# A packed-attention and two-MoE kernel: the order of the second MoE derived anew, and the sums that close each of its last two thirds moved

## The chip, the cores and the metric

The kernel runs on one core of a Trainium2 chip. The metric is the device time of one execution in microseconds (us), the median of several runs. Five engines work side by side: TensorE (PE, with its weight loads shown as PEld), VectorE (DVE), ScalarE (ACT), GpSimd (POOL) and SyncE (SP), which here only issues transfers (DMAs).

## The reference, cut to what matters

```
attn:  p_packed = softmax(p k^T / 8) v ;  x = softmax(q p_packed^T / 8) p_packed     (4 batches, 8 heads, 576 rows, 64)
moe:   h = x @ w_in ;  x = (h * cos(h)) @ w_out                                       (2304 x 512, d_ff 2048)
moe2:  p = domain_probs / sum ;  out = sum over 4 experts of  p[:, e] * (relu(x @ w1[e]) @ w2[e])    (F = 1024)
```

All of it is float32. To keep that accuracy on TensorE, each operand is split into a high and a low part, and each product is three matmuls (`mm3`, lines 204 to 207: high by high, high by low, low by high).

## The kernel before, in words

The work has two large stages. The first holds attention and the first MoE (up to about 395 us of the span). The second MoE fills the rest: 2304 tokens in three thirds (`NH = 3`), and 8 steps in each (`NU = 8`: 4 experts by 2 halves of 1024), 24 steps in all, numbered n. A step has two pieces on TensorE. `b_pair` (called twice, for j = 0 and 1) makes the hidden block by seven half-size products (`PRODUCTS`, Winograd's scheme), with additions on VectorE (L958), a relu that is multiplied with the experts' shares (L975), differences (L987), and a split into a high part (ACT, L667) and a low part (POOL, or VectorE where the planner puts it there; L658, `split`). The second product is `b_back` in the first third (512 columns to a matmul, evacuated in L1077), and `b_back2` in the other two: again seven products (`BACK`), each of 12 matmuls of 384 columns, named by their pair of operands. They add into five accumulators `v`, `w`, `c11`, `x53` and `x74`, each evacuated by one VectorE instruction over 768 columns (L1134), or by ACT for an accumulator's first product (L1132). w2's blocks that the last two thirds use are copied within the chip's main memory beforehand (`copy_w2`, L1318), since they are loaded again in each step (`kept_weights`).

At the end of a third (`u == NU - 1`), `final` (L1149) makes three sums on VectorE: x53 += v, w += x53, x74 += v, and `put` (L1156) stores c11, x53, w and x74.

The order of every engine's instructions is made by a planner (`Plan.run`). Each operation is entered with its engine, a duration in us, what it comes after, the buffers that it takes and uses, and for TensorE and SP a key. The planner walks through time: of the operations of an engine that can start first, it takes the one with the lowest key, and a TensorE operation whose key is more than 60 (`AHEAD`) above the lowest key left has to wait. A POOL operation with an `alt` can go to VectorE instead. Operations marked `port` and those of POOL never run at once in the plan. What comes out is one fixed list for each engine, and the chip runs each list in order. Three things scale the plan of the second MoE: `pl.slow` multiplies the durations on ACT, VectorE and POOL, `pl.late` is added to each transfer's end, and after a TensorE operation whatever depends on it may start 0.25 us later (`LATENCY`). The keys of a step are an offset of 100 n plus a number from `KEYS`: "a" for the 14 products of the two `b_pair`, "b" for those of `b_back` or `b_back2`, with lists of their own for the first step, the first third ("one"), the middle ("two"), the step before the end ("end") and the last products of all ("last").

Of the kernel before, what the change touches and what calls it, by code (L numbers as in the profile page):

```python
# [15 lines left out]
ALU = mybir.AluOpType  # L16
# [10 lines left out]
class Plan:  # L27
# [35 lines left out]
    def run(self):  # L63
# [15 lines left out]
        while done < len(self.ops):  # L79
# [55 lines left out]
            for x, w in [(x, fin) for x in o["next"]] + [(x, t) for x in o["then"]]:  # L135
                x["wait"] -= 1
                x["at"] = max(x["at"], w)
                if not x["wait"]:
                    todo[x["eng"]].append(x)
# [7 lines left out]
def tile_packed_attention_moe_moe2(ctx: ExitStack, tc: tile.TileContext, qT, kT, vk, pT, w_in, w_out, dp, w1, w2, out, out2):  # L147
# [16 lines left out]
    nc = tc.nc  # L164
# [59 lines left out]
    def dma(us, f, after=(), take=(), use=(), key=None, begun=()):  # L224
        return pl.op("SP", us, f, after, take, use, key, begun=begun)
# [873 lines left out]
    def b_back2(n, W, keys):  # L1099
# [4 lines left out]
        for i, (a, b, bank, new, acc, how) in enumerate(BACK):  # L1104
# [22 lines left out]
            def f_evac(ob=ob, ac=ac, acc=acc, how=how, first=first):  # L1127
                p = ob["t"][:, :, :TB]
# [4 lines left out]
                else:  # L1133
                    nc.vector.tensor_tensor(out=ac["t"], in0=ac["t"] if how == ALU.subtract else p,  # L1134
                                            in1=p if how == ALU.subtract else ac["t"], op=how)

            m = pl.op("PE", 2.08, f_mm, [g["ready"] for g in gl] + [w["ready"] for w in ws] + ([] if new else [free[bank]]),
                      [ob["slot"]] if new else [], [ob["slot"]] + [g["slot"] for g in gl] + [w["slot"] for w in ws], keys[i])
            free[bank] = ac["op"] = pl.op("ACT" if first else "DVE", 0.85 if first else 0.96, f_evac, [m, ac["op"]],
                                          [ac["slot"]] if first else [], [ob["slot"], ac["slot"]], keys[i] + 8)  # L1140
            last[0] = m
        if u < NU - 1:
            return

        def final(x, y, key):
            a, b = accs[h, x], accs[h, y]

            def f():
                nc.vector.tensor_tensor(out=a["t"], in0=a["t"], in1=b["t"], op=ALU.add)  # L1149

            a["op"] = pl.op("DVE", 0.95, f, [a["op"], b["op"]], [], [a["slot"], b["slot"]], key, port=True)

        def put(x, i, c, key):
            def f():
                t0 = (h - 1) * TH + c * TB
                nc.sync.dma_start(out=out2[i * 256:(i + 1) * 256, t0:t0 + TB].rearrange("(d p) n -> p d n", p=P),  # L1156
                                  in_=accs[h, x]["t"])

            dma(0.4 * MB2, f, [accs[h, x]["op"]], [], [accs[h, x]["slot"]], key)

        kf = keys[-1] + 20
        put("c11", 0, 0, kf)
        final("x53", "v", kf + 1), final("w", "x53", kf + 2), final("x74", "v", kf + 3)
        put("x53", 0, 1, kf + 10), put("w", 1, 1, kf + 11), put("x74", 1, 0, kf + 12)

# [9 lines left out]
    def share_ops():  # L1175
# [10 lines left out]
        def f_store():  # L1186
# [11 lines left out]
            'copy': [715.7, 22.6],  # L1198
# [7 lines left out]
            'keep': [117.2, -167, 205.3, 42.6],  # L1206
            'kept': [173.4, 203.5],
            'last': {'b': [39.4, 45.5, 37.7, 357.6, 51.2, 27.5, 165.9]},
# [27 lines left out]
            'one': {'a': [7.9, 13.2, 18.6, 61.7, 42.4, 68.2, 50.5, 39, 15.5, 61.8, 75.1, 71.4, 76.6, 72.1],  # L1236
                    'b': [14.1, 54.6, 76.5, 77.4, 55.9, 66.8]},
            'out0': [-122.9, -853.4],
            'two': {'a': [-11.2, 43, 29.3, 19.8, 20.5, 46.9, 7.1, 23, 52.9, 69, 21.4, 71.4, 100.2, 84.8],
                    'b': [8, 40.1, 58.9, 16.6, 79.4, 52.2, 103.3]}}  # L1240
# [86 lines left out]
    pl.slow, pl.late = 1.04, 0.8  # L1327
# [90 lines left out]
```

## Time and profile before

| what | us |
|---|---|
| median of 3 runs (lowest, highest) | 1152.04 (1151.27, 1152.55) |
| the profiled execution's own time | 1149.58 |
| its span, first to last instruction | 1147.8 |
| TensorE busy in the span | 1101.7 (96%) |
| VectorE, POOL, ACT busy | 835.3, 633.2, 493.4 |

The span is the stretch that the profile covers; the profiled execution took 1.8 us more than it, and 2.46 us less than the median. Busy TensorE time is modelled from the ends of pipelined matmuls, so a busy share near 100% can hide short gaps; how many matmuls start in a stretch tells more. In the lines of the profile, "idle before, releaser" is the time in which the engine stood still ahead of an instruction, and what it had waited for.

### The profile page before, as it was taken

How to read it: one execution, taken by the hardware profiler on the slowest of the kernel's cores; microseconds unless marked ns; L12 is line 12 of the kernel's file. 1: busy time of each engine (PE TensorE's matmuls, PEld its weight loads, DVE VectorE, ACT ScalarE, POOL GpSimd, SP SyncE). 2: the span in 40 equal slices, each digit the busy share in tenths (PEclk: the TensorE clock that was granted, in tenths of full speed). 3: DMA queues.
4: the chain of work that ended last, by engine and by line, in shares of the span. 5: the costliest groups of instructions: out<-in, count | busy, mean ns of one | idle time of the engine just before them, and what ended most of it. 6: DMA issues, size and time to landing. Idle time of an engine off the chain costs nothing.

```text
span 1147.8 us, 19120 instructions
## 1 busy us (share of the span) xinstructions
PE 1101.7 (96%) x7241; PEld 1032.5 (90%) x7241; DVE 835.3 (73%) x1244; ACT 493.4 (43%) x852; POOL 633.2 (55%) x477
## 2 busy tenths in 40 slices
PE   6689999999999999999999999999999999999997
PEld 4568999999999988888888889999999999999997
DVE  3798777567555677787777756888887768778776
ACT  3677655445444453244334434333334343333331
POOL 1454755435422775555566546656667767645553
PEclk8699999999999999999999999999999999999999
DMA  9673436433135859787866967676667876666653
GB/s 314 231 263 118 161 116 266 188 130 141 43 105 188 280 196 325 265 301 256 291 257 263 335 259 249 232 252 233 244 227 249 306 265 238 226 227 219 228 182 110
DMA packets 96815, 257.70 MB, mean 225 GB/s; under 512 B 10892, under 2 KB 34516, under 8 KB 94548
## 3 DMA queue, kind: packets, MB, share of 16 engines
q1 hardware_dynamic: 96724, 256.48, 63.1%
q8 instruction: 57, 0.93, 0.3%
q14 instruction: 34, 0.28, 0.1%
HBM read 192.97 MB, written 71.86 MB: 231 GB/s over the span
## 4 chain that ended last, share of the span: by engine, by line
PE 78%; DVE 8%; DMA 5%; issue 4%; ACT 3%; POOL 2%; SPq 0%; POOLq 0%; ACTq 0%; DVEq 0%
PE pa L205 26%; PE pa L207 25%; PE pa L206 25%; DMA w<-w 3%; PE pa L353 2%; DVE pa L958 1%; DVE s L755 1%; POOL aop L658 1%; POOL w L658 1%; DMA kt<-kT 1%; DVE acc L1134 1%; DVE p L958 1%; DVE u L975 0%; DVE oacc L1077 0%; DVE g L1010 0%
## 5 line engine op out<-in xcount | busy, mean ns | idle before, releaser
L205 PE MATMUL pa<-g,w 128*128 128x288 f32 (+1 forms) x960 | 303.6, 316 | 2.0 <-DVE acc L1134 0.8
L206 PE MATMUL pa<-g,w 128*128 128x288 f32 (+1 forms) x960 | 301.6, 314 | 1.2 <-POOL g L590 1.2
L207 PE MATMUL pa<-g,w 128*128 128x288 f32 (+1 forms) x960 | 301.2, 314 | 0.5 <-POOL w L297 0.5
L658 POOL TENSOR_TENSOR g<-u,g 128x384 fp32r<-128x384 f32 x157 | 171.5, 1105 | 140.3 <-ACT g L667 133.5
L205 PE MATMUL pa<-bop,aop 128*128 128x384 f32 x672 | 228.8, 341 | 9.3 <-DVE p L958 4.1
L207 PE MATMUL pa<-bop,aop 128*128 128x384 f32 x672 | 226.9, 338 | 1.5 <-POOL aop L658 1.5
L206 PE MATMUL pa<-bop,aop 128*128 128x384 f32 x672 | 226.3, 337 | 1.1 <-POOL bop L658 1.1
L205 PEld LDWEIGHTS pa<-g,w 128*128 128x128 f32 x960 | 180.1, 188 | 7.9 <-issue 2.4
L206 PEld LDWEIGHTS pa<-g,w 128*128 128x128 f32 x960 | 180.2, 188 | 1.9 <-POOL g L590 1.9
L207 PEld LDWEIGHTS pa<-g,w 128*128 128x128 f32 x960 | 180.4, 188 | 1.0 <-POOL w L297 1.0
L667 ACT ACTIVATE g<-u 128x384 fp32r<-128x384 f32 x192 | 97.2, 523 | 176.8 <-DVE u L987 134.9
L590 POOL TENSOR_TENSOR g<-t,g 128x576 fp32r<-128x576 f32 x64 | 93.2, 1470 | 118.8 <-ACT g L587 117.4
L205 PEld LDWEIGHTS pa<-bop,aop 128*128 128x128 f32 x672 | 126.1, 188 | 19.1 <-DVE p L958 6.1
L206 PEld LDWEIGHTS pa<-bop,aop 128*128 128x128 f32 x672 | 126.2, 188 | 3.0 <-POOL bop L658 1.4
L207 PEld LDWEIGHTS pa<-bop,aop 128*128 128x128 f32 x672 | 126.1, 188 | 2.2 <-POOL aop L658 2.2
L958 DVE TENSOR_TENSOR p<-pa,p 128x384 f32<-128x384 f32 x144 | 79.3, 554 | 41.4 <-PE pa L207 38.7
L1134 DVE TENSOR_TENSOR acc<-pa,acc 128x768 f32<-128x768 f32 x88 | 83.9, 954 | 32.6 <-PE pa L207 31.3
L658 POOL TENSOR_TENSOR w<-w 128x512 fp32r<-128x512 f32 x62 | 86.3, 1403 | 31.4 <-ACT w L705 31.2
L205 PE MATMUL pa<-at,m 128*128 128x288 f32 x256 | 78.7, 307 | 3.1 <-DVE t L583 2.0
L206 PE MATMUL pa<-at,m 128*128 128x288 f32 x256 | 77.5, 303 | 2.8 <-POOL at L658 2.8
L205 PE MATMUL pa<-w,g 128*128 128x512 f32 x192 | 75.9, 395 | 1.9 <-DVE oacc L1077 1.9
L207 PE MATMUL pa<-at,m 128*128 128x288 f32 x256 | 77.2, 301 | 0.0
(129 smaller groups left out, 1924.8 us busy)
## 6 DMA issues: line engine op xcount, KB each, us to landing
at<-at SPq DMA_DIRECT2D x16, 1152.0 KB, 5.3
raw<-w SPq DMA_DIRECT2D x32, 512.0 KB, 5.2
w<-w SPq DMA_DIRECT2D x64, 256.0 KB, 5.0
raw<-w_in SPq DMA_DIRECT2D x6, 1024.0 KB, 6.1
raw<-w_out SPq DMA_DIRECT2D x6, 1024.0 KB, 8.0
vt<-vk SPq DMA_DIRECT2D x8, 576.0 KB, 8.5
kt<-kT SPq DMA_DIRECT2D x8, 576.0 KB, 10.5
qt<-qT SPq DMA_DIRECT2D x8, 576.0 KB, 8.6
```

Of the source, the lines that this page charges most:

```text
L205: nc.tensor.matmul(o, lhsT=l(0), rhs=r(0), start=first, stop=False, skip_group_check=True)
L206: nc.tensor.matmul(o, lhsT=l(0), rhs=r(1), start=False, stop=False, skip_group_check=True)
L207: nc.tensor.matmul(o, lhsT=l(1), rhs=r(0), start=False, stop=last, skip_group_check=True)
L353: nc.tensor.matmul(o(e)[32 * q:32 * q + 32, :N], lhsT=l[64 * e:64 * e + 64, 32 * q:32 * q + 32], rhs=r(q // 2, q % 2)[64 * e:64 * e + 64], ...
L590: nc.gpsimd.tensor_tensor(out=s["g"][:, 1], in0=s["t"], in1=s["g"][:, 0].bitcast(F32), op=ALU.subtract)
L658: (nc.vector if on_vector else nc.gpsimd).tensor_tensor(out=dst[:, 1], in0=src, in1=dst[:, 0].bitcast(F32), op=ALU.subtract)
L667: nc.scalar.activation(r["t"][:, 0], src(), AF.Copy)
L755: nc.vector.tensor_tensor(out=t, in0=src(a, m)(), in1=src(b, m)(), op=o)
L958: nc.vector.tensor_tensor(out=s[o] if o in s else tmp(o), in0=s[x], in1=s[y], op=ALU.add)
L1134: nc.vector.tensor_tensor(out=ac["t"], in0=ac["t"] if how == ALU.subtract else p, in1=p if how == ALU.subtract else ac["t"], op=how)
```

## The change

Three things are edited. In the planner, a TensorE operation that depends on another TensorE operation may start as soon as that one's duration is over, without the 0.25 us, in the second MoE (`o["fair"]`). `pl.slow` goes from 1.04 to 1.08. And in `b_back2`, for the last step of a third, the sums and stores are entered in another place: c11 is stored after its last product (i = 2); after i = 5 come x74 += v, x53 += v, the store of x53, w += x53 and the store of w; the last entry, a22 by t4 (i = 6), is then added to x74 in two halves of 384 columns, each stored by itself. The keys of the second MoE and those of `copy`, `keep`, `kept` and `g` are new numbers. (Unchanged entries of `load` are left out below.)

```diff
--- before.py
+++ after.py
@@ -132,7 +132,7 @@
                 s["end"] = max(s["end"], fin)
                 if not s["users"]:
                     ends[s["tag"]].append(s["end"])
-            for x, w in [(x, fin) for x in o["next"]] + [(x, t) for x in o["then"]]:
+            for x, w in [(x, t + us if o["fair"] and eng == "PE" == x["eng"] else fin) for x in o["next"]] + [(x, t) for x in o["then"]]:
                 x["wait"] -= 1
                 x["at"] = max(x["at"], w)
                 if not x["wait"]:
@@ -1124,44 +1124,52 @@
                             return ws[0]["t"][:, x, k, d * P:(d + 1) * P]
                         mm3(ob["t"][:, d, :TB], l, lambda x: gl[k]["t"][:, x], new and k == 0, k == 1)
 
-            def f_evac(ob=ob, ac=ac, acc=acc, how=how, first=first):
-                p = ob["t"][:, :, :TB]
+            def f_evac(d=slice(0, 2), ob=ob, ac=ac, acc=acc, how=how, first=first):
+                p = ob["t"][:, d, :TB]
                 if first:
                     ac["t"] = (bp["ys"].tile([P, 2, TB], F32, tag="ys", name="acc", bufs=5) if acc == "x53" else
                                bp["raw"].tile([P, 2, 512], F32, tag="raw", name="acc", bufs=4)[:, :, :TB])
                     nc.scalar.activation(ac["t"], p, AF.Copy, scale=-1.0 if how == ALU.subtract else 1.0)
                 else:
-                    nc.vector.tensor_tensor(out=ac["t"], in0=ac["t"] if how == ALU.subtract else p,
-                                            in1=p if how == ALU.subtract else ac["t"], op=how)
+                    o = ac["t"][:, d]
+                    nc.vector.tensor_tensor(out=o, in0=o if how == ALU.subtract else p, in1=p if how == ALU.subtract else o,
+                                            op=how)
 
             m = pl.op("PE", 2.08, f_mm, [g["ready"] for g in gl] + [w["ready"] for w in ws] + ([] if new else [free[bank]]),
                       [ob["slot"]] if new else [], [ob["slot"]] + [g["slot"] for g in gl] + [w["slot"] for w in ws], keys[i])
+            last[0] = m
+            if u == NU - 1 and i == 6:
+                for d in range(2):
+                    ac["op"] = pl.op("DVE", 0.56, lambda d=d, f=f_evac: f(slice(d, d + 1)), [m, ac["op"]], [],
+                                     [ob["slot"], ac["slot"]], keys[i] + 8)
+                    put(h, acc, 1, 0, keys[i] + 12, d)
+                continue
             free[bank] = ac["op"] = pl.op("ACT" if first else "DVE", 0.85 if first else 0.96, f_evac, [m, ac["op"]],
                                           [ac["slot"]] if first else [], [ob["slot"], ac["slot"]], keys[i] + 8)
-            last[0] = m
-        if u < NU - 1:
-            return
-
-        def final(x, y, key):
-            a, b = accs[h, x], accs[h, y]
-
-            def f():
-                nc.vector.tensor_tensor(out=a["t"], in0=a["t"], in1=b["t"], op=ALU.add)
-
-            a["op"] = pl.op("DVE", 0.95, f, [a["op"], b["op"]], [], [a["slot"], b["slot"]], key, port=True)
-
-        def put(x, i, c, key):
-            def f():
-                t0 = (h - 1) * TH + c * TB
-                nc.sync.dma_start(out=out2[i * 256:(i + 1) * 256, t0:t0 + TB].rearrange("(d p) n -> p d n", p=P),
-                                  in_=accs[h, x]["t"])
-
-            dma(0.4 * MB2, f, [accs[h, x]["op"]], [], [accs[h, x]["slot"]], key)
-
-        kf = keys[-1] + 20
-        put("c11", 0, 0, kf)
-        final("x53", "v", kf + 1), final("w", "x53", kf + 2), final("x74", "v", kf + 3)
-        put("x53", 0, 1, kf + 10), put("w", 1, 1, kf + 11), put("x74", 1, 0, kf + 12)
+            if u == NU - 1 and i == 2:
+                put(h, "c11", 0, 0, keys[i] + 20)
+            if u == NU - 1 and i == 5:
+                final(h, "x74", "v", keys[i] + 9), final(h, "x53", "v", keys[i] + 10)
+                put(h, "x53", 0, 1, keys[i] + 20)
+                final(h, "w", "x53", keys[i] + 11)
+                put(h, "w", 1, 1, keys[i] + 21)
+
+    def final(h, x, y, key):
+        a, b = accs[h, x], accs[h, y]
+
+        def f():
+            nc.vector.tensor_tensor(out=a["t"], in0=a["t"], in1=b["t"], op=ALU.add)
+
+        a["op"] = pl.op("DVE", 0.95, f, [a["op"], b["op"]], [], [a["slot"], b["slot"]], key, port=True)
+
+    def put(h, x, i, c, key, d=None):
+        def f():
+            t0 = (h - 1) * TH + c * TB
+            dst = out2[i * 256:(i + 1) * 256, t0:t0 + TB].rearrange("(d p) n -> p d n", p=P)
+            t = accs[h, x]["t"]
+            nc.sync.dma_start(out=dst if d is None else dst[:, d], in_=t if d is None else t[:, d])
+
+        dma((0.4 if d is None else 0.2) * MB, f, [accs[h, x]["op"]], [], [accs[h, x]["slot"]], key)
 
     last, last_out = [None], [None]
 
@@ -1195,17 +1203,17 @@
                     [-93.3, -128.7, -68.2, -15.3, 13.3, 1421.4], [-83.4, 135.4, 82.9, 153.5, 102.6, 397.7]],
             'b': [[-144.5, 19.2, -205.9, -87.6], [-87.2, -44.5, 18, 62.9], [6.2, 37.5, 59.6, 71.8]],
             'blk': [206.7, 346.1, 218.8, 569.5, 339.1],
-            'copy': [715.7, 22.6],
-            'end': {'a': [1.9, 33.8, -41.8, -9.4, 62.6, 50.5, 58.2, 66, 50.3, 65.2, 164.6, 90.7, 98.5, 108.6],
-                    'b': [15.2, 19.6, 61.8, 6.4, -4.3, 137.2, 95.6]},
+            'copy': [698.4, -92.8],
+            'end': {'a': [7.4, 49.9, -96.8, -25.8, 10, 20.2, 59.3, 66, 69.2, 67.3, 153, 123.2, 167.4, 107.5],
+                    'b': [0.5, 22.1, 43, 35.4, -0.2, 147.4, 142.3]},
             'f': [[-837.7, -739.1, -526.4, -725.8], [-47.1, 45.5, 49.7, 46.5], [-3, 19.7, 90.8, 30.6],
                   [-10.1, 23.9, 43.8, 42.1]],
-            'first': {'a': [-99.6, -21.7, -44.8, 52.4, 61.8, -13.5, 44, -18.2, -13.9, 59.1, 88.2, 109.3, 65.9, 52.5]},
-            'g': [40.4, 18.4],
+            'first': {'a': [-115.8, -35.2, -26.6, 46, 88.4, 27.1, 37.9, 1.5, 6.9, 75.4, 52, 130.5, 41.1, 64.9]},
+            'g': [32.9, 10.4],
             'in0': [-1061.7, -368.5],
-            'keep': [117.2, -167, 205.3, 42.6],
-            'kept': [173.4, 203.5],
-            'last': {'b': [39.4, 45.5, 37.7, 357.6, 51.2, 27.5, 165.9]},
+            'keep': [42.4, -215.1, 270.7, 30.7],
+            'kept': [273.7, 232.3],
+            'last': {'b': [38.4, 14.6, 74.5, 338.2, 23.6, 158.4, 176]},
             'load': {'in': -1643.2,
...
@@ -1233,11 +1241,11 @@
...
             'm': [-906.3, -396.8, -49.1, 19.5, -23.6],
-            'one': {'a': [7.9, 13.2, 18.6, 61.7, 42.4, 68.2, 50.5, 39, 15.5, 61.8, 75.1, 71.4, 76.6, 72.1],
-                    'b': [14.1, 54.6, 76.5, 77.4, 55.9, 66.8]},
+            'one': {'a': [13.7, 29.8, 27.2, 55.9, 67.5, 52.9, 57.2, 49.8, 15.9, 46.6, 55, 74.9, 71.3, 108],
+                    'b': [14.1, 24.7, 62.7, 82.8, 51, 60.6]},
             'out0': [-122.9, -853.4],
-            'two': {'a': [-11.2, 43, 29.3, 19.8, 20.5, 46.9, 7.1, 23, 52.9, 69, 21.4, 71.4, 100.2, 84.8],
-                    'b': [8, 40.1, 58.9, 16.6, 79.4, 52.2, 103.3]}}
+            'two': {'a': [-13, 54.6, 26.2, 14.8, 19.7, 37.1, 7.9, 25.8, 57.9, 66.7, 23.7, 72.1, 93.6, 99.6],
+                    'b': [6.3, 17.6, 62.4, 14.6, 84.7, 69.3, 110.8]}}
 
     def kv(n, vtag):
         load_kv(n, vtag, KEYS["load"]["k%d" % n], KEYS["load"]["v%d" % n])
@@ -1324,7 +1332,7 @@
         copy_w2(u)
     share_ops()
     ops_a = list(pl.ops)
-    pl.slow, pl.late = 1.04, 0.8
+    pl.slow, pl.late = 1.08, 0.8
     late = [o for o in ops_a if o["f"].__qualname__.split(".")[-3] in ("a_front", "a_back")]
     mid = [o for o in ops_a if o["f"].__name__ == "f_mm" and "a_front" in o["f"].__qualname__]
     early = [o for o in ops_a if not any(o is x for x in late)]
```

## Rows read from the trace of the kernel before

**Rows 1.** Page, part 1: busy time, share and instructions of TensorE.
```profile
PE 1101.7 (96%) x7241; PEld 1032.5 (90%) x7241; DVE 835.3 (73%) x1244; ACT 493.4 (43%) x852; POOL 633.2 (55%) x477
```
**Rows 2.** Busy time by stretch: us, engines' busy (instructions), PEclk, DMA, GB/s.
```profile
200.00:240.00 40.00, 40.00 (x317) 37.99 (x316) 20.40 (x26) 18.45 (x27) 16.41 (x11) 1.00 0.45 169
...
680.00:1120.00 440.00, 433.09 (x2453) 427.06 (x2452) 344.23 (x513) 162.40 (x311) 274.87 (x235) 1.00 0.68 240
```
**Rows 3.** What TensorE waited for, 395 to 660 us: total, times, longest.
```profile
PE pa L205 <- DVE p L958: 2.2, 6, 0.7
PE pa L205 <- DVE oacc L1077: 1.9, 3, 1.1
PE pa L207 <- POOL aop L658: 1.5, 2, 0.8
PE pa L206 <- POOL bop L658: 1.1, 1, 1.1
```
**Rows 4.** What TensorE waited for, 680 to 1120 us.
```profile
PE pa L205 <- DVE pa L958: 2.3, 4, 1.2
PE pa L205 <- DVE u L975: 2.0, 7, 0.6
PE pa L205 <- DVE p L958: 1.3, 2, 0.7
PE pa L205 <- DVE acc L1134: 0.8, 1, 0.8
```
**Rows 5.** Timeline of VectorE at the end: start, us, line, tiles, idle before.
```profile
1137.32 0.96 DVE L1134 TENSOR_TENSOR acc<-pa,acc 128x768 f32<-128x768 f32 x1 [1.12 <-PE pa L207]
1139.40 0.96 DVE L1134 TENSOR_TENSOR acc<-pa,acc 128x768 f32<-128x768 f32 x1 [1.12 <-PE pa L207]
1140.40 0.96 DVE L1149 TENSOR_TENSOR acc<-acc 128x768 f32<-128x768 f32 x1
1141.49 0.96 DVE L1134 TENSOR_TENSOR acc<-pa,acc 128x768 f32<-128x768 f32 x1
1142.48 1.95 DVE L1149 TENSOR_TENSOR acc<-acc 128x768 f32<-128x768 f32 x2
```
**Rows 6.** Page, part 6: issues of stores, KB each, median us to landing.
```profile
y<-yacc SPq DMA_DIRECT2D x24, 192.0 KB, 2.3
...
out<-acc SPq DMA_DIRECT2D x8, 384.0 KB, 3.0
```
**Rows 7.** Durations (ns, min/median/max) by tile; the last by form, mean ns.
```profile
L958 DVE TENSOR_TENSOR p<-pa,p x144: 537/557/560, 400.3 to 1126.6; 128x384 f32<-128x384 f32 x144
L987 DVE TENSOR_TENSOR u<-p,u x64: 541/557/1581, 660.0 to 1130.9; 128x384 f32<-128x384 f32 x64
...
L658 POOL TENSOR_TENSOR w<-w 128x512 fp32r<-128x512 f32 x62 | 86.3, 1403 | 31.4 <-ACT w L705 31.2
```
**Rows 8.** Timeline of POOL, VectorE and TensorE around one wait, 1076 to 1080 us.
```profile
1076.47 2.84 POOL L658 TENSOR_TENSOR w<-w 128x512 fp32r<-128x512 f32 x2 [3.54 <-ACT w L705]
...
1076.84 1.33 DVE L658 TENSOR_TENSOR g<-u,g 128x384 fp32r<-128x384 f32 x1 [1.63 <-ACT g L667]
...
1078.10 0.94 DVE L1134 TENSOR_TENSOR acc<-acc,pa 128x768 f32<-128x768 f32 x1
...
1078.97 0.55 DVE L958 TENSOR_TENSOR pa<-pa,p 128x384 f32<-128x384 f32 x1
...
1079.57 0.44 PE L205 MATMUL pa<-bop,aop 128*128 128x384 f32 x1 [1.23 <-DVE pa L958]
```
**Rows 9.** The copies of w2 (timeline of SP, landing), the attention load, its use.
```profile
174.98 2.17 SPq L1318 DMA_DIRECT2D w<-w  x3
...
DMA to landing us min/median/max: 7.4/10.5/14.0
...
at<-at SPq DMA_DIRECT2D x16, 1152.0 KB, 5.3
...
222.19 0.40 PE L205 MATMUL pa<-at,m 128*128 128x288 f32 x1
```

## The prediction, made before the changed kernel ran

> **What bounds the kernel now.** I first read the busy times of the page: TensorE is busy in 96% of the span [rows 1], so time can only come from where it stands still, or from what follows its last matmul. Then the busy times by stretch: in the first stage it is busy for all of 40 us, and the granted clock is full [rows 2]; nothing is to be had there. In the second MoE it isn't full: between 680 and 1120 us 2453 matmuls start [rows 2]. In an unbroken run 12 of them take 2.08 us, the distance of two evacuations at the end [rows 5], so one takes 0.1733, and 2453 take 425.1 us of the 440. So 14.9 us are lost in 15 steps, one us in each.
>
> The waits say to whom. In that stretch the four largest groups are all behind VectorE, 6.4 us in 14 waits [rows 4]; in the first third the four largest are 6.7 us in 12, 4.1 of it behind VectorE and 2.6 behind POOL [rows 3]. The waits show too little: a matmul is drawn about 0.34 us long though the next could start after 0.173, and the first matmul after a wait is 0.44 instead of 0.34 [rows 8], so I add 0.27 to each. The first third then loses at least 6.7 + 12 x 0.27 = 9.9 us, and the stage some 25. The last thing read is the end: after the last matmul VectorE makes one evacuation and two sums, from 1141.49 to 1144.43 [rows 5], and the last store follows.
>
> **The change part by part.** The sum is made against the profiled execution (1149.58, its span 1147.8); the median lies 2.46 above that, and I add the same difference.
>
> *The sums and halves at the end: 0.* If the product a22 by t4 were the last on TensorE, its two halves alone would stand behind it: two instructions over 384 columns, 0.557 each [rows 7], about 1.14 with their starts, in place of 2.94 [rows 5], and a store of 192 KB, which lands in 2.3 us, in place of one of 384 KB in 3.0 [rows 6]: 1.8 + 0.7 = 2.5 us less. But the keys say otherwise. In "last" the entry i = 6 has 176, and i = 3 (w1 by t1, into x53) has 338.2. The planner holds back a TensorE operation that is more than 60 above the lowest key left, so i = 3 stays behind i = 6, as it did before (357.6 and 165.9): rows 5 show it, one sum (x74 += v) ahead of the last evacuation and two (x53 += v, w += x53) after. Both of these need x53, so after the change, too, one evacuation and two sums follow the last matmul. The halves cost 2 x 0.557 - 0.96 = 0.15 us of VectorE, which waits 1.12 us for TensorE there [rows 5], and one more store, issued while SP waits for those sums: nothing. If that cover were gone, the end would be 0.15 us later. At the end of the second third i = 6 is the last by its key, but TensorE goes on with the next step there; the stores' new places on SP's queue I set at 0, since none of the four largest waits is for a transfer [rows 4]. So 0, from -2.5 to +0.2.
>
> *The copies of w2: 0.* Their keys fall from 698 by 93 for each block, where they rose from 716. Before, they went in groups between the attention loads, the first three at 175 us [rows 9]; now most of the eight stand ahead of the next attention load on SP's queue. Three took up to 14.0 us to land, 4.7 each, so eight are through by 175 + 37.6 = 212.6, and the load behind them, 5.3 us, by 218. It is first used at 222.2 [rows 9]. The cover is 4 us of buffered data, and TensorE has no gap there [rows 2]. A late load would cost what it exceeds that by: 2 us if each copy took 5.5 us. Nothing in the first stage gains.
>
> *The new order: -4.3.* This is the part that decides, and no row shows an order that has not run, so I bound it. The two corrections go one way: in the plan VectorE and POOL get slower and TensorE faster. Take the chain behind one wait [rows 8]: a split, an evacuation and an addition, planned at 0.53 + 0.96 + 0.56 = 2.05 us; 4% more of that is 0.08. A pair of chained products gets 0.25. So a plan that meets its times has up to 0.33 us more slack on the chip at such a place, and the 26 waits of rows 3 and 4 are at most 1.2 us long, 0.3 to 0.8 in the mean of most groups. Taking 0.33 off every one gives -8.6, the lower bound. The upper bound is that the new lists bring as many new waits as they remove, or more: the second rival below prices it at +5 as its middle. I take half of the gain, 4.3, because the two kinds of cause are about equally frequent: short waits, which slack cures, and ones like that of rows 8, which it doesn't. There the split on VectorE took 1.33 us where 0.53 was planned, since POOL was splitting a weight at the same time; 0.08 does nothing against 0.8. The difference goes to the waits that are next: on VectorE's `u` (L975), 0.3 us each [rows 4].
>
> What the durations show speaks on both sides. The mean of POOL's split of a weight is 1.403 [rows 7], and 1.3 x 1.08 is 1.404, where 1.04 gives 1.352. But VectorE's addition takes 0.557 [rows 7] and is now planned at 0.605. The difference `u` takes 0.557 in the middle and 1.581 at most [rows 7]: what is long is the meeting with POOL, not the work.
>
> Sum: -4.3 + 0 + 0, so 1145.3 for the profiled execution and 1147.7 for the median.
>
> **The rivals.**
>
> *No change, because the excess was a lock and the plan already had it.* The operations that read two tensors of SBUF are planned apart from POOL's (`port`), so a longer time for each counts twice what rows 7 show as long. Then 1.08 is margin in the wrong place, the search trades one set of short waits for another, and the time is 1152.0. The Trainium skill has the rule, in "SBUF — State Buffer", section "SBUF: two separate sides": the port pair that VectorE and GpSimd share is "an exclusive lock, not a bandwidth split", and the loser is blocked for the whole instruction. The trace agrees in rows 8, with 1.33 us for a split planned at 0.53; by the rule alone the sum would be 0 instead of -4.3. For this rival: that 0.04 is small beside 0.8. Against: the 0.25 us on TensorE has nothing to do with the port.
>
> *Slower: splits go to VectorE ahead of evacuations.* A POOL operation with an `alt` moves to VectorE when that is earlier in the plan, and with each POOL split 4% longer that choice comes more often. Its place is the middle steps, in the pattern of rows 8: a split on VectorE, blocked by POOL, an evacuation behind it in the queue, then the addition on which TensorE waits. That wait is there 4 times in 15 steps, 2.3 us [rows 4], with 0.27 each 0.85 us. If it came in ten of the steps, six more would cost 5.1 us: 1157.1. It decides from the point at which VectorE has no gap left to catch up: it is busy 344 of 440 us [rows 2], 78%. For it: that share, and that every list is one fixed order. Against: VectorE is planned 4% longer as well.
>
> *The end is shortened after all*, because i = 6 comes last: -2.5 more, 1145.2. Against it stands the key 338.2.
>
> **How the numbers follow.** About 0.2%, 2.3 us, is what a measurement of this kernel can tell from no change. The forecast gets 0.46 (0.43 faster, 0.03 within), the shorter end 0.07 (faster), no change 0.22 (0.04 faster, 0.15 within, 0.03 slower), the slower case 0.25 (0.22 slower, 0.03 within). That makes 0.54 faster, 0.21 within and 0.25 slower. The range goes from 1140.5, near the forecast's lower bound with the shorter end (1152.0 - 8.6 - 2.5 = 1140.9), to 1156.0, short of the slower case's middle, which leaves some 0.1 above and little below. The likeliest case's own range is 1143.4 to 1150.
>
> **What would show it.** Right: the number of matmuls between 680 and 1120 us above 2453 by about 12, fewer waits behind VectorE, TensorE without a gap at 200 to 240 us, and still one evacuation and two sums after the last matmul, the halves ahead of it. Wrong: as many or more waits (the count at or below 2453), more splits on VectorE ahead of L1134, an end with the two halves alone, or a wait on the attention load near 222 us.

## The result, and the profile after

The changed kernel takes 1137.46 us in the median of five runs (1135.14 to 1139.8), the kernel before 1152.4 in the same series: 0.9877 of it, with a 95% interval of 0.9862 to 0.9892. That is 15 us less. The forecast was 4.3 less, and the range ended 3 us above the result. The profiled execution is the slowest of the five: 1139.8, its span 1138.0.

The first part of the changed kernel's page, to be held against [rows 1]:

```profile
PE 1098.4 (97%) x7241; PEld 1034.1 (91%) x7241; DVE 804.2 (71%) x1223; ACT 490.9 (43%) x852; POOL 656.9 (58%) x500
```

Its busy times by stretch (the first two answer to [rows 2], columns as there; the other three are 120 us each of the first, second and last third):

```profile
680.00:1120.00 440.00, 435.37 (x2483) 432.49 (x2482) 329.22 (x505) 159.71 (x311) 292.40 (x253) 1.00 0.71 238
...
200.00:240.00 40.00, 40.00 (x317) 37.99 (x316) 20.97 (x27) 18.14 (x27) 16.21 (x10) 1.00 0.37 130
...
520.00:640.00 120.00, 119.03 (x594) 106.68 (x593) 82.47 (x131) 52.42 (x101) 77.32 (x54) 1.00 0.74 273
720.00:840.00 120.00, 120.00 (x688) 119.70 (x687) 93.90 (x145) 41.15 (x83) 75.69 (x67) 1.00 0.70 241
960.00:1080.00 120.00, 120.00 (x688) 119.64 (x687) 91.72 (x139) 41.30 (x82) 80.84 (x73) 1.00 0.71 236
```

The same three stretches of the kernel before:

```profile
520.00:640.00 120.00, 116.82 (x578) 103.41 (x577) 88.58 (x132) 48.28 (x94) 72.19 (x50) 1.00 0.74 268
720.00:840.00 120.00, 119.22 (x681) 118.29 (x679) 100.11 (x147) 41.90 (x82) 72.55 (x62) 1.00 0.68 236
960.00:1080.00 120.00, 117.11 (x664) 115.29 (x663) 94.88 (x143) 40.45 (x80) 69.36 (x62) 1.00 0.67 236
```

The number behind TensorE's first time is how many matmuls started. At 0.1733 us each, 120 us hold 692 of them where all have 384 columns (in the first third some have 512). The steady steps of the last two thirds are now full: 688 and 688, from 681 and 664. Between 680 and 1120 us 2483 start instead of 2453, and what is lost there is 440 - 2483 x 0.1733 = 9.7 us, from 14.9. The waits of TensorE from 395 to 660 us, and then from 680 to 1120 us, answer to [rows 3] and [rows 4]:

```profile
PE pa L205 <- DVE p L958: 2.1, 3, 0.8
PE pa L205 <- DVE pa L958: 1.1, 1, 1.1
PE pa L206 <- DVE bop L658: 0.9, 1, 0.9
PE pa L205 <- DVE g L1010: 0.3, 1, 0.3
...
PE pa L206 <- POOL bop L658: 1.7, 1, 1.7
PE pa L205 <- DMA w<-q7w: 1.2, 1, 1.2
PE pa L205 <- DMA w<-q1w: 0.8, 2, 0.6
PE pa L205 <- DMA w<-q0w: 0.6, 1, 0.6
PE pa L205 <- DVE u L975: 0.4, 2, 0.2
```

Of the 6.4 us behind VectorE in [rows 4], 0.4 is left. The waits that remain are for loads and for a token block (`bop`), 3.5 of the 4.7 us between the second and the last third. In the profiled execution the second stage begins at 384.7 us, 1.7 later than before, its first to its last matmul takes 746.5 us in place of 758.1, and 6.8 us follow the start of the last in place of 6.7: 1.7 - 11.6 + 0.1 = -9.8, the difference of the spans. (The profiled execution of the kernel before is 2.5 us shorter than its median, so the traces show less of the gain than the medians do.) The other four executions of the series are 1.8 to 4.7 us shorter than this one; no trace shows where.

The end, VectorE's timeline, to be held against [rows 5] (the evacuation in L1135 was L1134, the sums in L1161 were L1149):

```profile
1128.40 0.96 DVE L1161 TENSOR_TENSOR acc<-acc 128x768 f32<-128x768 f32 x1
1129.48 1.02 DVE L1135 TENSOR_TENSOR acc<-pa,acc 128x384 f32<-128x384 f32 x2
1131.57 0.96 DVE L1135 TENSOR_TENSOR acc<-pa,acc 128x768 f32<-128x768 f32 x1 [1.06 <-PE pa L207]
1132.56 1.95 DVE L1161 TENSOR_TENSOR acc<-acc 128x768 f32<-128x768 f32 x2
```

The two halves stand ahead of the last product, and one evacuation and two sums behind it, as the keys said.

### The profile page after: what moved, and what is told of

Same layout as the page of the kernel before. It is cut to its first block, busy times and chain, and to the rows that moved or that the text cites. A ratio compares the mean times of both kernels' runs of the same rounds, so it can differ in the third digit from the quotient of the medians.

```text
span 1138.0 us, 19115 instructions
## 1 busy us (share of the span) xinstructions
PE 1098.4 (97%) x7241; PEld 1034.1 (91%) x7241; DVE 804.2 (71%) x1223; ACT 490.9 (43%) x852; POOL 656.9 (58%) x500
## 3 DMA queue, kind: packets, MB, share of 16 engines
q1 hardware_dynamic: 96756, 256.49, 64.9%
## 4 chain that ended last, share of the span: by engine, by line
PE 84%; DVE 6%; DMA 5%; ACT 2%; issue 1%; POOL 1%; SPq 0%; ACTq 0%; DVEq 0%
PE pa L205 28%; PE pa L207 27%; PE pa L206 27%; PE pa L353 2%; DMA w<-q1w 1%; DMA kt<-kT 1%; DMA w<-q7w 1%; DVE s L755 1%; DVE p L958 1%; DMA w<-q0w 1%; DMA bop<-y 1%; DMA q5w<-w2s 0%; DMA q6w<-w2s 0%; DVE mx L377 0%; PE pa L409 0%
## 5 line engine op out<-in xcount | busy, mean ns | idle before, releaser
L658 POOL TENSOR_TENSOR g<-u,g 128x384 fp32r<-128x384 f32 x172 | 183.8, 1081 | 125.7 <-ACT g L667 117.1
L1135 DVE TENSOR_TENSOR acc<-pa,acc 128x768 f32<-128x768 f32 (+1 forms) x90 | 84.2, 937 | 38.4 <-PE pa L207 37.9
L658 POOL TENSOR_TENSOR w<-w 128x512 fp32r<-128x512 f32 x64 | 89.4, 1406 | 27.5 <-ACT w L705 27.4
```

The source lines that it names most:

```text
L658: (nc.vector if on_vector else nc.gpsimd).tensor_tensor(out=dst[:, 1], in0=src, in1=dst[:, 0].bitcast(F32), op=ALU.subtract)
L1135: nc.vector.tensor_tensor(out=o, in0=o if how == ALU.subtract else p, in1=p if how == ALU.subtract else o, op=how)
```

## The experiments

Which of the plan's parts brings the time? Theory A: the longer planned durations (the factor, `pl.slow`), by the room that they leave. Theory B: only keys and numbers together. Theory C: the new keys, as a better set. Theory D: the 0.25 us taken out. Later theories (E to G) are named where they are tested. Each run is timed against the kernel before, on the same chip as the others of its group. The table has the medians and, from the profile of each, the matmuls started in the three stretches shown above ("0.25" says whether the plan keeps that time between dependent TensorE operations).

| kernel | keys | factor | 0.25 | median us (before) | 520-640 | 720-840 | 960-1080 |
|---|---|---|---|---|---|---|---|
| before | old | 1.04 | yes | 1152 | 578 | 681 | 664 |
| changed | new | 1.08 | no | 1137.5 (1152.4) | 594 | 688 | 688 |
| old_keys_slow108 | old | 1.08 | yes | 1159.5 (1152.2) | 594 | 679 | 670 |
| new_keys_slow104 | new | 1.04 | yes | 1158.3 (1152.2) | 593 | 674 | 667 |
| after_slow104 | new | 1.04 | no | 1154.6 (1152.2) | 577 | 689 | 675 |
| after_with_025 | new | 1.08 | yes | 1150.1 (1152.2) | 590 | 677 | 671 |
| old_keys_no025 | old | 1.04 | no | 1152.3 (1152.3) | 577 | 689 | 689 |
| old_keys_both | old | 1.08 | no | 1162.8 (1152.6) | 591 | 685 | 677 |
| old_keys_link_j0 | old | 1.04 | one link | 1144.3 (1152.1) | 578 | 690 | 681 |
| old_keys_link_j1 | old | 1.04 | other link | 1149.1 (1152.1) | 579 | 684 | 661 |
| after_old_sums | new | 1.08 | no | 1141.4 (1152.3) | 595 | 687 | 688 |
| after_splits_free | new | 1.08 | no | 1154.4 (1152.3) | 580 | 671 | 680 |
| after_old_copy_keys | new | 1.08 | no | 1138.4 (1152.6) | 595 | 687 | 688 |
| after_x74_last | new | 1.08 | no | 1136.5 (1152.3) | 595 | 689 | 685 |
| after_x53_between | new | 1.08 | no | 1136.7 (1152.6) | 595 | 689 | 687 |

Windows at fixed times miss what lies between them. Counted by matmuls instead, from start to start, the traces of the second stage (4032 matmuls, 96 early ones still of the first MoE) divide into four pieces of work. The first 1416 matmuls end with the last product of the first third, and they hold the same work in every kernel. The next 1104 are steady steps of the second third. The 336 after them are the joint, in which the second third ends and the last begins. The rest is the last third. Times in us:

| kernel | first 1416 | next 1104 | joint, 336 | last third | all |
|---|---|---|---|---|---|
| before | 289.2 | 196.9 | 60.8 | 211.2 | 758.1 |
| changed | 282.7 | 193.7 | 63.4 | 206.7 | 746.5 |
| old_keys_slow108 | 291.1 | 196.0 | 69.0 | 210.2 | 766.2 |
| new_keys_slow104 | 290.1 | 197.3 | 61.2 | 214.0 | 762.5 |
| after_slow104 | 290.8 | 192.8 | 69.2 | 210.8 | 763.6 |
| after_with_025 | 283.8 | 197.3 | 64.9 | 211.7 | 757.8 |
| old_keys_no025 | 289.0 | 194.5 | 69.1 | 207.7 | 760.4 |
| old_keys_both | 290.8 | 195.1 | 67.8 | 217.5 | 771.3 |
| old_keys_link_j0 | 288.2 | 193.8 | 59.7 | 211.5 | 753.2 |
| after_splits_free | 289.2 | 196.6 | 61.3 | 212.5 | 759.6 |

So 6.5 of the 11.6 us are won in the first third, 3.2 and 4.6 in the steps of the other two, and the joint loses 2.6. The two gains have different causes. The first third is short only where the new keys and 1.08 come together, with the 0.25 us or without. The second third is short where the 0.25 us is gone from one link (the runs on links below show which), whatever the keys and the factor. Only after_splits_free, taken up below, has all of this and loses both gains.

**The parts one by one.** The first four runs put back or apply one part of the plan.

*The factor alone, on the kernel before:*

```diff
-    pl.slow, pl.late = 1.04, 0.8
+    pl.slow, pl.late = 1.08, 0.8
```

> The kernel before with one edit: the planner's factor 1.08 in place of 1.04; keys, sums and TensorE's 0.25 us as before. Theory A (room: the longer durations leave VectorE and POOL time on the chip, whatever the keys): most of the waits go although no key was searched for this factor, 1140 to 1146 us, and fewer than 10 waits of TensorE shown between 680 and 1120 us (15 before). Theory B (a searched set of keys and its factor belong together): the old keys give a worse order under the new factor, 1150 to 1158 us.

Measured: 1.006 of before (1.0038 to 1.0081), 1159.5 us, even a little above theory B's range; 11 waits are shown from 680 to 1120 us. Theory A falls. The window of the first third fills, 594 from 578, but the first third as a whole takes 1.9 us longer than before, and the joint 8.2.

*The new keys alone, on the kernel before:*

```diff
-            'copy': [715.7, 22.6],
+            'copy': [698.4, -92.8],
...
-            'two': {'a': [-11.2, 43, 29.3, 19.8, 20.5, 46.9, 7.1, 23, 52.9, 69, 21.4, 71.4, 100.2, 84.8],
+            'two': {'a': [-13, 54.6, 26.2, 14.8, 19.7, 37.1, 7.9, 25.8, 57.9, 66.7, 23.7, 72.1, 93.6, 99.6],
...
```

> The kernel before with the new keys alone: factor 1.04, TensorE's 0.25 us and the place of the sums as before. Theory A (room): with 1.04 the tight spots come back, 1148 us or more, and 12 or more waits shown between 680 and 1120 us. Theory C (the new keys are simply a better set): 1135 to 1141 us.

Measured: 1.0054 (1.0038 to 1.007). The keys are not a better set by themselves: theory C falls. Theory A's numbers hold (13 waits are shown from 680 to 1120 us, 8.6 us in all), but theory B would say the same.

*The factor put back in the changed kernel:*

```diff
-    pl.slow, pl.late = 1.08, 0.8
+    pl.slow, pl.late = 1.04, 0.8
```

> The changed kernel with the factor put back to 1.04, all else as changed. Theory A: the waits come back in the steady steps too; matmuls started from 720 to 880 us fall from 923 to about 912, the count of the kernel before, and the time is 1148 us or more. Theory C: 1135 to 1141 us. Theory D (it is the 0.25 us taken out on TensorE): as C, since that stays in.

Measured: 1.003 (1.0016 to 1.0045). The time, 1154.6 us, is theory A's and refutes what C and D gave; the place isn't A's: from 720 to 880 us 915 matmuls start. (The text above has 923 and 912 for the kernels after and before; their traces have 917 and 906.) Against the changed kernel 8.0 us are lost in the first third, 4.1 in the last, and 5.8 in the joint, where TensorE waits 5.9 us at a stretch for a token block (the last section shows it).

*The 0.25 us put back in the changed kernel:*

```diff
-            for x, w in [(x, t + us if o["fair"] and eng == "PE" == x["eng"] else fin) for x in o["next"]] + [(x, t) for x in o["then"]]:
+            for x, w in [(x, fin) for x in o["next"]] + [(x, t) for x in o["then"]]:
```

> The changed kernel with the 0.25 us between dependent TensorE operations put back in the plan, all else as changed. Theory D (that edit carries the gain): 1147 us or more. Theories A and C: within 3 us of the changed kernel's 1137.5.

Measured: 1150.1 us, 0.9985 of before (0.9968 to 1.0002): 12.6 of the 15 us are gone with this one line, and in the traces 11.3 of the 11.6. Theory D's number holds, theories A and C fall. The first third keeps its gain (283.8); what it won is lost again in the other pieces. The steady steps show it:

```profile
720.00:840.00 120.00, 119.40 (x677) 117.53 (x676) 96.81 (x142) 40.50 (x80) 71.04 (x65) 1.00 0.70 236
960.00:1080.00 120.00, 117.89 (x671) 116.67 (x670) 93.33 (x141) 40.02 (x80) 71.19 (x64) 1.00 0.69 234
```

**The 0.25 us with the old keys.** The same line applied to the kernel before:

```diff
-            for x, w in [(x, fin) for x in o["next"]] + [(x, t) for x in o["then"]]:
+            for x, w in [(x, t + us if o["fair"] and eng == "PE" == x["eng"] else fin) for x in o["next"]] + [(x, t) for x in o["then"]]:
```

> The kernel before with one edit: the 0.25 us between dependent TensorE operations taken out of the plan; old keys, factor 1.04, old sums. In its list s1 by t1 follows s3 by t3 at once, as in the changed kernel. Theory D (that link carries most of the gain with any keys): 1140 to 1146 us, and the steady steps of the second third lose little: 915 or more matmuls started from 720 to 880 us (906 before). Theory B (factor, link and keys belong together): 1150 to 1158 us, like the two runs that changed one of them.

```profile
720.00:840.00 120.00, 120.00 (x689) 119.91 (x688) 94.67 (x144) 41.02 (x81) 76.02 (x68) 1.00 0.70 235
960.00:1080.00 120.00, 120.00 (x689) 120.00 (x688) 96.88 (x144) 41.46 (x82) 72.21 (x67) 1.00 0.70 243
...
860.00:930.00 70.00, 62.66 (x343) 60.85 (x343) 52.31 (x74) 25.18 (x46) 46.16 (x36) 0.98 0.71 251
```

The last stretch in the kernel before:

```profile
860.00:930.00 70.00, 68.71 (x387) 67.11 (x386) 51.63 (x79) 28.78 (x52) 51.66 (x43) 1.00 0.79 280
```

Measured: 1.0 (0.9985 to 1.0016). Both theories get half: the steady steps are as full as in the changed kernel, with the old keys and the old factor (917 matmuls from 720 to 880 us), but from 860 to 930 us, between the second and the last third, 343 matmuls start where the kernel before has 387. At 0.1733 us each that is 7.6 us, more than the 5.9 that the pieces before and behind the joint gained in the last two thirds.

*Both numbers with the old keys:*

```diff
-    pl.slow, pl.late = 1.04, 0.8
+    pl.slow, pl.late = 1.08, 0.8
...
+            for x, w in [(x, t + us if o["fair"] and eng == "PE" == x["eng"] else fin) for x in o["next"]] + [(x, t) for x in o["then"]]:
```

> The kernel before with the old keys and old sums, but both of the plan's numbers as changed: factor 1.08 and no 0.25 us. Theory F (the 0.25 us governs the steady steps of the last two thirds whatever the keys, the factor those of the first third, the search of the keys only the joints between thirds and the ends): matmuls started from 720 to 840 and from 960 to 1080 us 685 or more each (681 and 664 before), from 520 to 640 us 590 or more (578 before), and yet no gain in time, 1150 to 1160 us, since the joints are worse than in either kernel. Theory G (even the steady steps need searched keys): 680 or fewer in at least one of the last two stretches.

Measured: 1.01 (1.0068 to 1.0132), 591, 685 and 677. Theory F holds in two of the three stretches; in the last third theory G does, so the keys count there too. They count in the first third as well, which as a whole takes 1.6 us longer than before (290.8), its full window notwithstanding. The time is worse than F's range.

**Which link.** A step has two kinds of dependent pairs on TensorE, s2 by t2 behind a11 by b11, and s1 by t1 behind s3 by t3. If the planner frees only the first kind of the 0.25 us in the changed kernel, its list for TensorE stays as it is with 0.25; if it frees only the second kind, the list is the changed kernel's. So it is the second, and with the old keys I freed it for one call of a step at a time:

```diff
+            o["j"] = j if bank == "d" and after else None
...
-            for x, w in [(x, fin) for x in o["next"]] + [(x, t) for x in o["then"]]:
+            for x, w in [(x, t + us if o["fair"] and eng == "PE" and x.get("j") == 0 else fin) for x in o["next"]] + [(x, t) for x in o["then"]]:
```

> The kernel before with the 0.25 us taken out only for the link from s3 by t3 to s1 by t1 of the first call of a step (j = 0). In the list s1 by t1 then comes before s2 by t2, and s2 by t2 of the second call and a12 by b21 change places further on. If this call's link carries the steady steps: 685 or more matmuls from 720 to 840 and from 960 to 1080 us (681 and 664 before, 689 and 689 with both links free), and about 6 us less than before minus what the end of the second third loses, 1147 to 1151 us. If the other call's does: 681 and 664 as before.

> The kernel before with the 0.25 us taken out only for that link of the second call (j = 1). The list of TensorE in a steady step differs in one exchange: s1 by t1 right behind s3 by t3, ahead of a12 by b21. If this link carries the steady steps: 685 or more in both stretches and 1145 to 1149 us, since the plan's own stand-stills are those of the kernel before. If the other call's does: about 681 and 664, 1152 us.

```profile
720.00:840.00 120.00, 120.00 (x690) 120.00 (x689) 93.70 (x144) 40.44 (x81) 75.44 (x67) 1.00 0.68 235
960.00:1080.00 120.00, 118.80 (x681) 118.47 (x680) 94.05 (x143) 40.83 (x81) 77.05 (x69) 1.00 0.69 236
```

That is the first call's; the second call's follows:

```profile
720.00:840.00 120.00, 119.44 (x684) 118.86 (x683) 98.04 (x147) 41.90 (x82) 73.28 (x62) 1.00 0.69 237
960.00:1080.00 120.00, 116.61 (x661) 114.99 (x661) 91.96 (x141) 40.54 (x81) 71.41 (x63) 1.00 0.68 235
```

The first call's link gives 0.9933 (0.9909 to 0.9957), 1144.3 us: 7.8 us less than before by the medians and 4.9 in the traces, with old keys, the old factor and the old sums. That is better than the expected range. But its count in the last third, 681, is short of 685: the second third and the joint gain, the last third as a whole does not (211.5 us, 211.2 before). The second call's gives 0.9983 (0.9965 to 1.0), which is not clear of no change, and leaves the last third as it was. With the first link free, s1 by t1 moves ahead of s2 by t2; s2 by t2 of the second call moves up too, and `b_back2`'s a12 by b21 into the place that it left. Which of these moves counts no run shows. The planner's lists point to the first: in six steps of the second third, about 697 to 874 us, the lists of after_with_025 and of the changed kernel have the other two moves in common, and differ in the first and in one more exchange (s1 by t1 of the second call ahead of w2 by t2).

**Splits on VectorE.** The planner's charge for that is taken away in the second MoE:

```diff
-                    cost = lambda o: 8 * (o["table"] not in (None, table)) if eng == "ACT" else 15 * (o["eng"] != eng)
+                    cost = lambda o: 8 * (o["table"] not in (None, table)) if eng == "ACT" else (0 if o["fair"] else 15) * (o["eng"] != eng)
```

> The changed kernel with the planner's charge for putting a split on VectorE (15) taken away in the second MoE. TensorE's order in the steady steps is unchanged, but from 720 to 880 us 15 splits stand on VectorE in place of 9, and from 960 to 1080 us 10 in place of 2. Theory E (splits on VectorE, blocked by POOL ahead of an evacuation, make the waits): matmuls started in those two stretches fall from 917 and 688 to about 908 and 670, 1146 us or more. Rival (their number does not matter, only the order): 914 and 685 or more there, and a time that is later by what the ends of the thirds lose, 1140 to 1144 us.

Measured: 1154.4 us, 1.0012 (0.9992 to 1.0031), with 900 matmuls from 720 to 880 us and 680 from 960 to 1080. Theory E holds in direction. From 720 to 840 us the order on TensorE is that of the changed kernel in both traces, and 17 fewer matmuls start (671). In the last third the order is another, against what was expected, so the 8 that are missing there are not the splits' alone. The splits that stand on VectorE (L658) from 960 to 1080 us, by the groups of instructions; first the kernel before:

```profile
L658 DVE TENSOR_TENSOR g<-u,g 128x384 fp32r<-128x384 f32 x12 | 11.0, 919 | 5.0 <-ACT g L667 5.0
```

The same view of the changed kernel:

```profile
L658 DVE TENSOR_TENSOR g<-p,g 128x384 fp32r<-128x384 f32 x1 | 1.3, 1258 | 0.0
L658 DVE TENSOR_TENSOR g<-u,g 128x384 fp32r<-128x384 f32 x1 | 0.5, 545 | 0.0
```

And of after_splits_free:

```profile
L658 DVE TENSOR_TENSOR g<-u,g 128x384 fp32r<-128x384 f32 x10 | 8.2, 820 | 0.5 <-ACT g L667 0.5
```

Their number alone doesn't decide: old_keys_no025 has 7 there and starts 689, old_keys_both has none and starts 677. The run also lost 6.5 us in the first third, and in the last steps before the end, so its time is not theory E's alone.

**The sums, the end and the copies.** The old place of the sums, in the changed kernel:

```diff
-            if u == NU - 1 and i == 6:
-                for d in range(2):
...
+        kf = keys[-1] + 20
+        put("c11", 0, 0, kf)
+        final("x53", "v", kf + 1), final("w", "x53", kf + 2), final("x74", "v", kf + 3)
+        put("x53", 0, 1, kf + 10), put("w", 1, 1, kf + 11), put("x74", 1, 0, kf + 12)
```

> The changed kernel with the sums and stores of a third back in their old place and whole (no halves), all else as changed. My prediction's reasoning (the sums and halves are worth nothing by themselves): within 3 us of 1137.5 in the steady steps; but the keys were made for the other list, so under theory B the end of each third gets worse and the time is 1142 to 1150 us. If the halves shorten the end, the stretch behind the last matmul grows by up to 2.5 us; by my reading it stays at three VectorE instructions.

Measured: 1141.4 us, 0.9901 (0.9882 to 0.992). The steady steps stay full, and 6.7 us lie behind the start of the last matmul, where the kernels before and after have 6.7 and 6.8. The 4 us are lost mostly in the last steps before the end. Whether the place of the sums costs them, or keys that were made for the other list, this run can't tell apart.

*One key for the last products, in two versions:*

```diff
-            'last': {'b': [38.4, 14.6, 74.5, 338.2, 23.6, 158.4, 176]},
+            'last': {'b': [38.4, 14.6, 74.5, 138.2, 23.6, 158.4, 176]},
```

> The changed kernel with one key: in the last products of all, 138.2 for w1 by t1 in place of 338.2, so that a22 by t4 is the last product on TensorE and its two halves alone stand behind it. By the prediction's sum for that case the stretch behind the last matmul gets 2.5 us shorter (two additions of 0.55 us and a store of half the size): 1135 us in place of 1137.5. Rival: the end is set by the stores on SP's queue, then no change.

```diff
-            'last': {'b': [38.4, 14.6, 74.5, 338.2, 23.6, 158.4, 176]},
+            'last': {'b': [38.4, 14.6, 74.5, 167, 23.6, 158.4, 176]},
```

> The changed kernel with one key: 167 for w1 by t1 in the last products, between w2 by t2 (158.4) and a22 by t4 (176). Then x53 is evacuated and x74 += v is done while TensorE still works, and behind the last matmul stand two halves and one sum, some 2.1 us on VectorE in place of 2.9; the last store is half as large, 0.7 us. 1136 us, 1.5 below the changed kernel. Rival (SP's stores or the end of the program set it): as the changed kernel, 1137.5.

VectorE's timeline at the end of the first version, whose last matmul starts at 1128.22 in a span of 1134.8:

```profile
1127.51 1.83 DVE L1161 TENSOR_TENSOR acc<-acc 128x768 f32<-128x768 f32 x2
1129.25 0.55 DVE L1135 TENSOR_TENSOR acc<-pa,acc 128x384 f32<-128x384 f32 x1
1129.72 0.95 DVE L1161 TENSOR_TENSOR acc<-acc 128x768 f32<-128x768 f32 x1
1130.59 0.55 DVE L1135 TENSOR_TENSOR acc<-pa,acc 128x384 f32<-128x384 f32 x1
```

And of the second, whose last matmul starts at 1127.97 in a span of 1133.8:

```profile
1127.25 0.96 DVE L1161 TENSOR_TENSOR acc<-acc 128x768 f32<-128x768 f32 x1
1128.35 0.56 DVE L1135 TENSOR_TENSOR acc<-pa,acc 128x384 f32<-128x384 f32 x1
1128.82 0.95 DVE L1161 TENSOR_TENSOR acc<-acc 128x768 f32<-128x768 f32 x1
1129.68 0.55 DVE L1135 TENSOR_TENSOR acc<-pa,acc 128x384 f32<-128x384 f32 x1
```

The stretch behind the start of the last matmul is 6.8 us in the changed kernel, 6.6 in the first version and 5.8 in the second: 0.2 and 1.0 us less. In the first the halves do not stand alone: two sums are still running when the last matmul is through, and a third stands between the halves. Nor does the smaller last store show: from the end of VectorE's last instruction to the end of the span it is 3.5 us in the changed kernel, 3.7 and 3.5 in the two versions. The medians are 1136.5 (0.9856 of before, 0.9836 to 0.9875) and 1136.7 (0.9863, 0.984 to 0.9886). Both beat the kernel before; from the changed kernel's 1137.5 neither can be told apart.

*The copies at their old place:*

```diff
-            'copy': [698.4, -92.8],
+            'copy': [715.7, 22.6],
```

> The changed kernel with the two numbers for the copies of w2 put back (715.7, 22.6). The prediction's term for the copies is 0: within 2 us of 1137.5, TensorE without a gap from 200 to 240 us in both. Rival (the copies' earlier place clears the way for later loads): 1140 us or more.

Measured: 1138.4 us, 0.9878 (0.9853 to 0.9904), as the changed kernel, and TensorE is busy for all of 200 to 240 us in both; the second stage takes 746.6 us in this trace and 746.5 in the changed kernel's. The copies are worth nothing.

## Why the prediction was wrong

**Right:** what bounds the kernel, and where the time went: steady steps of the second MoE, waits behind VectorE. The sums and halves did not shorten the end, and the order there is the one that the key 338.2 foretold. The copies cost and gained nothing.

**Wrong, the step that failed: "The new order: -4.3", with "Taking 0.33 off every one gives -8.6, the lower bound".** The direction was right and the term was mis-sized: it measured -15 by the medians, and -11.6 between the first and the last matmul of the second stage in the profiled executions. More than half of that, 6.5 us, lies in the first third, where its 12 waits at 0.33 were 4.0 at most.

- I took the 0.25 us for slack that shortens each wait by as much. It isn't slack: it decides which product comes next. Freed for a single link, with everything else as before, it gave 7.8 us (old_keys_link_j0), and put back in the changed kernel it cost 12.6 (after_with_025). The waits were not shortened by 0.33 each: of the 14 behind VectorE in [rows 4], 2 are left.
- So the lower bound was wrong too. The waits times 0.33 is no bound on a new order; the lost time is, and the prediction had it: some 25 us in the stage. A range that began there would have held the result.
- "I take half": I held waits like the one of rows 8, a split on VectorE behind POOL, to be out of reach. Those splits became fewer instead (12 to 2 from 960 to 1080 us), and the group that rows 8 belong to, behind VectorE's `pa`, is no longer among the waits from 680 to 1120 us. How much of the gain is due to this is not shown: old_keys_both has no such split there and is slower than before.
- I added the effects of factor and link as if each gave its share. Alone, the three gave 1.006 (factor), 1.0054 (keys) and 1.0 (0.25 us) of the time before, and the factor put back, or the 0.25 us, in the changed kernel lost 17 and 12.6 us. Keys fit one plan. With 1.08 or without the 0.25 us the old keys lose 7 to 8 us in the joint between the second and the last third; the new keys with both lose 2.6 there.

**The rivals.** "No change, because the excess was a lock": refuted by the result. The long splits are in the trace after as before: of the two splits above one takes 1258 ns, while POOL is splitting too, and the other 545, while it isn't. But the list now puts fewer splits on VectorE. By the rule of the Trainium skill, "SBUF — State Buffer", section "SBUF: two separate sides", alone the sum was 0; the trace agrees with the lock in that split of 1258 ns, but the time did not stay. "Slower, splits go to VectorE": the mechanism is real (after_splits_free: 17 matmuls or 2.9 us in the 120 us where TensorE's order is the same), the direction was wrong: the longer durations sent splits to POOL, whose instructions rose from 477 to 500 (498 with the factor alone, 480 with the new keys alone). "The end is shortened after all": it wasn't, and where I made a22 by t4 the last product it was 0.2 us, not 2.5, since sums stand ahead of the halves and between them; the second version gave 1.0.

**Not settled:** what the new keys and 1.08 do in the first third that neither does alone. Of the nine kernels with 1.08 eight start 590 to 595 matmuls from 520 to 640 us (after_splits_free 580), of the six with 1.04 five only 577 to 579, but new_keys_slow104 starts 593; and the first third as a whole is short only with both. And why the exchange of two products spares the waits is shown by its effect alone.

## What to carry to other kernels

Where an order is computed from a plan, a latency in the plan that the chip doesn't show is not a small error. From 720 to 840 us of the changed kernel no two matmuls start more than 0.23 us apart, chained products among them; the planned 0.25 us on one link moved a few products in each step, and taking it out there was worth 7.8 of the 15 us. The numbers of the plan and the keys searched under them belong together; test such a change as a whole, and look at the steady part and the joints apart, since one can eat what the other gains. The bound on what a new order can give is the time lost, not the number of waits times the slack that each gets.

## What the runs showed of the hardware that was not expected

A long gap of TensorE can cost more than it is long. In after_slow104 TensorE has this wait, the longest from 680 to 1120 us:

```profile
PE pa L206 <- POOL bop L658: 5.9, 1, 5.9
```

It ends at 895 us. The busy times of that kernel around it, in steps of 5 us:

```profile
885.00:890.00 5.00, 4.33 (x25) 4.01 (x23) 3.74 (x7) 2.52 (x4) 2.98 (x3) 1.00 0.98 340
890.00:895.00 5.00, 0.00 (x0) 0.00 (x0) 3.44 (x3) 0.52 (x1) 5.00 (x4) 0.71 0.87 345
895.00:900.00 5.00, 4.10 (x12) 3.60 (x13) 2.46 (x4) 2.72 (x5) 3.48 (x4) 0.50 0.07 27
900.00:905.00 5.00, 5.00 (x24) 4.85 (x23) 2.59 (x4) 0.42 (x1) 2.24 (x2) 0.77 0.21 52
905.00:910.00 5.00, 5.00 (x30) 5.00 (x29) 4.38 (x8) 2.16 (x6) 3.33 (x3) 1.00 0.20 56
```

The third column from the end is the granted clock: full (2.4 GHz) up to 890 us, it falls to the lower of the two levels (0.50, 1.2 GHz) while TensorE waits. Single matmuls show when it is back:

```profile
901.23 0.52 PE L206 MATMUL pa<-g,w 128*128 128x384 f32 x1
901.55 0.52 PE L207 MATMUL pa<-g,w 128*128 128x384 f32 x1
...
902.78 0.34 PE L206 MATMUL pa<-bop,aop 128*128 128x384 f32 x1
902.95 0.34 PE L207 MATMUL pa<-bop,aop 128*128 128x384 f32 x1
```

Up to 902.2 us they start 0.32 us apart, then 0.17. In the two windows from 895 to 905 us 36 matmuls start where 57.7 fit: 3.8 us are lost there. TensorE stands still for 0.9 of them (the end of the long wait, and a second one of 0.7 us), so some 2.9 us, an estimate from these rows, are the lower clock's, on top of the wait of 5.9.

The clock also falls below full in the windows of 860 to 930 us of three other runs whose joint was bad: 0.95 in old_keys_slow108, 0.98 in old_keys_no025 and in old_keys_both, where the longest single waits were 2.5, 2.8 and 2.4 us, with others near them. A wait of 3.0 us there in after_with_025 left the clock at full, and so did the changed kernel's longest, 1.7 us.
